# A fused attention and expert kernel: expert 0's second half takes its relus on the scalar engine, both halves are turned sooner, two small routing steps move

## The chip, the cores and the metric

One Trainium2 chip, of which the kernel uses one core. The metric is the time of one execution in microseconds on the device (us); lower is better. A core has a TensorE (PE: matrix products; PEld is its weight load), a VectorE (DVE), a ScalarE (ACT), a GpSimd (POOL) and a SyncE (SP), which here issues most transfers. Each engine takes its instructions in the order of its own queue.

## The reference, cut to what matters

```python
for t in range(S):                                   # B, H, S, D = 4, 8, 768, 48
    state = f[:, :, t, :, None] * state + np.einsum('bhd,bhe->bhde', k[:, :, t], v[:, :, t])
    y[:, :, t] = np.einsum('bhd,bhde->bhe', q[:, :, t], state)
x = y as (3072, 384)
h = x @ w_in                                         # (384, 2048)
x = (h - np.tanh(h)) @ w_out                         # (2048, 384)
out = x.copy()
xc = x[x @ w_skip > 0]                               # the rows that are computed
e_idx = np.argmax(xc @ w_gate, axis=1)               # one of 8 experts for each row
gate_w = the softmax probability of that expert
for e in range(8):
    h = np.maximum(xc[e_idx == e] @ w1[e], 0.0)      # (384, 1024), relu
    y[e_idx == e] = gate_w * (h @ w2[e])             # (1024, 384)
out[rows computed] = xc + y
```

## The kernel before, in words

Everything is fp32 in and out. The 3072 tokens are 24 blocks of 128 rows, or 12 pairs of blocks. Attention, the first product (`gemm1`), tanh and the second product (`gemm2`, L779) run interleaved for some 550 us. Their order is set by a planner that has a cost and a due time for every step, and for the last pairs by loops written by hand. In the last pair, the second block's last seven second products are kept for the end: the loop over `n` and `f` at `last = [route_now(...)...]` runs them with `gemm2(NB - 1, f, (1,))`. Each is three matmuls of 128x384.

**Routing.** As a block's rows are done they are copied from PSUM into a tile `pay` (`finish1`, L788). Scores for the eight experts and the skip score follow, and `place` (from L800) turns them into a row number of a buffer `xs` in HBM, in which every expert has a region: `choose` gives the one-hot row `oh`, the token's own number is copied from `ids` into `pay` (L803), two matmuls count the rows before this one (`pp`, L807 and L808, with `run` as the counts of all earlier blocks), `run` is increased by `oh` (L809), and on the DVE `sl`, `df` and `dst` (L813 to L821) make the address. The POOL then issues the scatter of `pay` into `xs` (L822). For the last two blocks, 22 and 23, `route_now` does the scores by transposes and products on the TensorE, between other work.

**Experts.** An expert takes up to 256 rows, read from `xs` into `xa` by `load_xa` (issued on SP, L996). Experts 1 to 7 split their weights and rows into a high and a low part, so that a product is three fast matmuls (`up` L1269, `down` L1293); the high part is a copy on the ScalarE (L352), the low part a subtract on the DVE or the POOL (L353). Expert 0 comes while the weights of expert 1 are being split, so it uses plain fp32 and goes in two halves of 128 rows, written (0,0) and (0,1):

- `half_turn` (L1013): three transposes (px, L1017) of the half's rows, then a copy to `xt` on the ScalarE (L1019).
- `half_up` (L1021), for eight f: three matmuls (L1027) into `eh`, a buffer of a pool `ph` that has two, then a relu on the DVE (L1030). The text calls such three matmuls an eh group.
- `half_down` (L1032), for eight f: a matmul of h with the second weight into `eo` (L1036).
- `deliver` (L1002): gate and residual on the DVE (`yo`, L1007), and a scatter into `out` (L999).

In time: half (0,0) is turned after the main stage's last product and after the copy of block 23 into `pay`; its eight half_ups have pieces of block 23's routing between them; `load_xa` for half (0,1) follows the last scatter. During the eight half_downs of (0,0), `split_raw(1, f)` splits expert 1's eight pieces of weight: eight copies on the ScalarE, six subtracts on the DVE, two on the POOL. Then come `deliver`, the turning of half (0,1), and its eight half_ups, with a `turn` of expert 1's rows (two transposes L1259 into a buffer `pt` of two, copy L1260, subtract on the DVE L1261) after f = 2, 4 and 6. From there expert follows expert.

Of the kernel before, what the change touches and what calls it, by code (L numbers as in the profile page):

```python
# [12 lines left out]
I32 = mybir.dt.int32  # L13
U32 = mybir.dt.uint32
AF = mybir.ActivationFunctionType
ALU = mybir.AluOpType
# [81 lines left out]
def decay_attention_moe_kernel(  # L98
# [14 lines left out]
    nc = tc.nc  # L113
    P = 128
    B, H, T, D = q.shape
    NT, DM = out.shape
# [8 lines left out]
    NF2 = F2 // P  # L125
# [58 lines left out]
    ids = cpool.tile([P, NU], I32, tag="ids", name="ids")  # L184
# [3 lines left out]
    run = cpool.tile([P, E], BF16, tag="run", name="run")  # L188
# [85 lines left out]
    def choose(pool, lg, tag):  # L274

        mx = pool.tile([P, 8], F32, tag="mx", name=f"mx{tag}")
        mi = pool.tile([P, 8], U32, tag="mi", name=f"mi{tag}")
        sm = pool.tile([P, 8], F32, tag="sm", name=f"sm{tag}")
        nm, rt, xf, sv = (sm[:, i : i + 1] for i in range(4))
        nc.vector.max(mx, lg[:, :E])  # L280
        nc.vector.tensor_scalar(nm, mx[:, 0:1], -1.0, None, op0=ALU.mult)
        ex = pool.tile([P, E], F32, tag="ex", name=f"ex{tag}")
        nc.scalar.activation(ex, lg[:, :E], AF.Exp, bias=nm, accum_out=sv)
        nc.vector.max_index(mi, mx, lg[:, :E])
        nc.vector.tensor_scalar(rt, lg[:, E : E + 1], 0.0, None, op0=ALU.is_gt)
        nc.vector.tensor_copy(xf, mi[:, 0:1])
        oh = pool.tile([P, E], BF16, tag="oh", name=f"oh{tag}")
        nc.vector.tensor_scalar(oh, iota8, xf, rt, op0=ALU.is_equal, op1=ALU.mult)
        return oh, rt, sv

    def gate_weight(gw, sv):
        nc.vector.tensor_scalar(gw, sv, 1e-9, None, op0=ALU.add)
        nc.vector.reciprocal(gw, gw)
# [10 lines left out]
    yp = pctx.enter_context(tc.tile_pool(name="yp", bufs=2, space=PSUM))  # L304
# [145 lines left out]
    def begun(u):  # L450
        blk, half = divmod(u, 2)
        return NF * blk - LEAD + 6 * half - (NF // 2 if 2 < blk <= LASTB else 0)
# [317 lines left out]
    def gemm2(blk, f, rows=(0, 1)):  # L770
        t = gt[blk, f]
        if f == first_f[blk]:
            for s in range(2):
                home, tag, w = (yp, "yp", 512) if blk in homes else (po_pool, "po", DM)
                po[blk, s] = home.tile([P, w], F32, tag=tag, name=f"po{blk}_{s}")[:, :DM]
        for s in rows:
            ss = slice(s * P, (s + 1) * P)
            for n, (a, w) in enumerate(((0, uhi), (0, ulo), (1, uhi))):
                nc.tensor.matmul(  # L779
                    po[blk, s], lhsT=t[:, a, ss], rhs=w[:, f], start=(f == first_f[blk] and n == 0),  # L780
                    stop=(f == last_f[blk] and n == 2),
                )
# [3 lines left out]
    def finish1(u):  # L786
        pt = pay[u] = rpool.tile([P, RW], F32, tag="pay", name=f"pay{u}", bufs=NPAY)
        nc.scalar.activation(pt[:, :DM], po[divmod(u, 2)], AF.Copy)  # L788

    def finish2(u):  # L790
        c, b = divmod(u, B)
        r0 = b * T + c * P
        nc.sync.dma_start(out[r0 : r0 + P, :], pay[u][:, :DM])

    def finish(blk, rows=(0, 1)):
        for s in rows:
            finish1(2 * blk + s)
            finish2(2 * blk + s)

    def place(pt, lg, u):  # L800

        oh, rt, sv = choose(rpool, lg, f"{u}")
        nc.vector.tensor_copy(pt[:, DM + 1 : DM + 2].bitcast(I32), ids[:, u : u + 1])  # L803
        yield
        yield
        pp = pa.tile([P, 512], F32, tag="pa", name=f"pp{u}")[:, :E]
        nc.tensor.matmul(pp, lhsT=tri_s, rhs=oh, start=True, stop=False)  # L807
        nc.tensor.matmul(pp, lhsT=ones, rhs=run, start=False, stop=True)  # L808
        nc.vector.tensor_tensor(run, run, oh, ALU.add)  # L809
        gate_weight(pt[:, DM : DM + 1], sv)  # L810
        yield
        sl = rpool.tile([P, E], F32, tag="sl", name=f"sl{u}")
        nc.vector.tensor_tensor(sl, pp, ebase, ALU.add)  # L813
        df = rpool.tile([P, 1], F32, tag="df", name=f"df{u}")
        s2 = rpool.tile([P, E], F32, tag="s2", name=f"s2{u}")
        nc.vector.tensor_tensor_reduce(
            out=s2, in0=sl, in1=oh, scale=1.0, scalar=float(OOB), op0=ALU.mult, op1=ALU.add, accum_out=df
        )
        c, b = divmod(u, B)
        di = dst[:, b * NCH + c : b * NCH + c + 1]  # L820
        nc.vector.scalar_tensor_tensor(out=di, in0=rt, scalar=-float(OOB), in1=df, op0=ALU.mult, op1=ALU.add)  # L821
        nc.gpsimd.indirect_dma_start(  # L822
            xs[:, :],
            bass.IndirectOffsetOnAxis(ap=di, axis=0),
            pt[:, :],
            None,
            bounds_check=E * NT - 1,
            oob_is_err=False,
        )
        yield  # L830

    def route(u):
        pt = pay[u]
        lg = rpool.tile([P, E + 1], F32, tag="lg", name=f"lg{u}")
        yield from dots(rpool, pt[:, :DM], f"{u}", wb, lg)
        yield from place(pt, lg, u)
# [130 lines left out]
    def split_raw(e, n):  # L967
        if e >= E:
            return
        raw = raws.pop((e, n))  # L970
        if n == 0:
            experts[e] = [wpool.tile([P, 2, KT, F2], F32R, tag="W", name=f"w1_{e}"), None]
        if n == NEC:
            experts[e][1] = wpool.tile([P, 2, NF2, DM], F32R, tag="W", name=f"w2_{e}")
        if n < NEC:
            a, w = experts[e][0], F2 // NEC
            fs = slice(n * w, (n + 1) * w)
            split(a[:, 0, :, fs], a[:, 1, :, fs], raw, nc.vector)
        else:
            a, r = experts[e][1], NF2 // NEC  # L980
            fs = slice((n - NEC) * r, (n - NEC + 1) * r)
            split(a[:, 0, fs], a[:, 1, fs], raw, nc.vector if e == 1 and n % 2 else nc.gpsimd)
        if e > 1:
            load_raw(e + 1, n)

    xas, xts, hts, eo = {}, {}, {}, {}
# [3 lines left out]
    def load_xa(e, rows=(0, 1)):  # L990
        if e < E:
            if e not in xas:
                xas[e] = epool.tile([P, 2, RW], F32, tag="xa", name=f"xa{e}", bufs=NXA)
            a, b = rows[0], rows[-1] + 1
            r0 = e * NT
            nc.sync.dma_start(xas[e][:, a:b], xs[r0 + a * P : r0 + b * P, :].rearrange("(s p) w -> p s w", p=P))  # L996
# [17 lines left out]
    def half_turn(e, s, pool, tag):  # L1014
        px = pool.tile([P, KT, P], F32, tag=tag, name=f"px{e}_{s}")
        for i in range(KT):
            nc.tensor.transpose(px[:, i], xas[e][:, s, i * P : (i + 1) * P], ident)  # L1017
        xts[e, s] = epool.tile([P, KT, P], F32, tag="xt", name=f"xt{e}_{s}")
        nc.scalar.activation(xts[e, s], px, AF.Copy)  # L1019

    def half_up(e, s, f):  # L1021

        ph = ph_pool.tile([P, P], F32, tag="ph", name=f"eh{e}_{s}_{f}")
        w = F2 // NEC
        n, fs = f * P // w, f * P % w
        for i in range(KT):
            nc.tensor.matmul(ph, lhsT=raws[e, n][:, i, fs : fs + P], rhs=xts[e, s][:, i], start=(i == 0), stop=(i == KT - 1))  # L1027
        if f % 4 == 0:
            hts[e, s, f // 4] = epool.tile([P, 4, P], F32, tag="h", name=f"h{e}_{s}_{f}", bufs=NH)
        nc.vector.tensor_scalar(hts[e, s, f // 4][:, f % 4], ph, 0.0, None, op0=ALU.max)  # L1030

    def half_down(e, s, f):  # L1032
        if f == 0:
            eo[e, s] = po_pool.tile([P, DM], F32, tag="po", name=f"eo{e}_{s}")
        n, m = divmod(f, NF2 // NEC)
        nc.tensor.matmul(  # L1036
            eo[e, s], lhsT=hts[e, s, f // 4][:, f % 4], rhs=raws[e, NEC + n][:, m], start=(f == 0), stop=(f == NF2 - 1)
        )
# [71 lines left out]
    for u in range(NU):  # L1110
        blk, half = divmod(u, 2)
        e = EARLIEST + 6 * u if u < FIRST else begun(u) - 8
# [116 lines left out]
    for n, f in enumerate(range(NF - SPLIT, NF)):  # L1229
        gemm2(NB - 1, f, (1,))  # L1230
        if n in (1, 3):
            next(last[0])
    finish(NB - 1, (1,))
    half_turn(0, 0, yp, "yp")
    next(last[0])
    for f in range(NF2):
        half_up(0, 0, f)
# [3 lines left out]
    for e in range(1, NXA):  # L1241
        load_xa(e)
    for f in range(NF2):
        half_down(0, 0, f)
        split_raw(1, f)
    deliver(0, (0,))
# [3 lines left out]
    pt_pool = mctx.enter_context(tc.tile_pool(name="ptp", bufs=2, space=PSUM))  # L1250
# [73 lines left out]
        nc.vector.tensor_copy(flag, fl)  # L1324
        yield

    half_turn(0, 1, pt_pool, "pt")
    for f in range(NF2):
        half_up(0, 1, f)
        if f in (2, 4, 6):  # L1330
# [8 lines left out]
    for g in range(NF2, E * NF2 + LAG):  # L1339
        e, f = divmod(g, NF2)  # L1340
# [276 lines left out]
```

## Time and profile before

| | us |
|---|---|
| median of three runs | 719.68 (718.21 to 721.0) |
| the profiled execution, its own time | 718.64 |
| its span | 716.8 |
| busy time: PE | 690.8 (96%) |
| busy time: PEld | 622.3 (87%) |
| busy time: DVE | 496.2 (69%) |
| busy time: ACT | 360.5 (50%) |
| busy time: POOL | 294.9 (41%) |

The span is what the hardware profiler saw between the first and the last instruction of one execution; what the execution takes beside it is 1.84 us. All times in rows are microseconds from the start of the span, unless marked ns. A matmul's end is modelled and overlaps the next one's start, so that starts are the better guide.

### The profile page before, as it was taken

To read this page: it belongs to the slowest core of one execution; us is meant where nothing else is said; L and a number is where in the kernel's file an instruction comes from. 1 tells how busy PE (TensorE), PEld (TensorE's weight loads), DVE (VectorE), ACT (ScalarE), POOL (GpSimd) and SP (SyncE) were. 2 spreads that over 40 slices of the span, in tenths; PEclk is the share of its full clock that TensorE was granted. 3 is DMA by queue.
4 is the path that set the end of the run, shared out by engine and by line. 5 is a ranking of instruction groups with operands and counts; after the bars stand their busy time and mean duration, and the time that the engine had idled before them with its cause. 6 is when DMAs were issued, how large, how long until landed. Compare 5 with 4: busy or idle time off the path is not lost.

```text
span 716.8 us, 15504 instructions
## 1 busy us (share of the span) xinstructions
PE 690.8 (96%) x5690; PEld 622.3 (87%) x5690; DVE 496.2 (69%) x1388; ACT 360.5 (50%) x882; POOL 294.9 (41%) x340
## 2 busy tenths in 40 slices
PE   7899989999999999999999999999999899999995
PEld 4688889988888888888889888999999689999995
DVE  3988997689878686784857669469784745555531
ACT  4877665564456453464454444443434435555530
POOL 4446444223333434334335334335543314555551
PEclk9999999999999999999999999999999999999998
DMA  9994345842232131222310120033003566666500
GB/s 224 231 258 128 123 165 145 251 88 46 54 76 56 35 88 32 54 51 55 68 24 29 40 58 17 7 122 117 13 29 104 179 222 227 218 213 216 176 16 25
DMA packets 147499, 76.71 MB, mean 107 GB/s; under 512 B 113288, under 2 KB 142617, under 8 KB 147286
## 3 DMA queue, kind: packets, MB, share of 16 engines
q1 hardware_dynamic: 142550, 64.18, 33.2%
q0 software_dynamic: 4768, 11.39, 4.4%
q8 instruction: 47, 0.77, 0.4%
q14 instruction: 38, 0.31, 0.1%
q10 hardware_dynamic: 96, 0.05, 0.0%
HBM read 61.60 MB, written 15.86 MB: 108 GB/s over the span
## 4 chain that ended last, share of the span: by engine, by line
PE 75%; DVE 6%; issue 5%; POOL 2%; ACT 1%; DMA 0%; POOLq 0%; ACTq 0%; DVEq 0%
PE po L779 24%; PE ph L737 22%; PE eh L1269 8%; PE eo L1293 8%; PE py L581 3%; PE ps L543 2%; POOL gs L762 2%; PE py L528 2%; PE eh L1027 1%; PE py L588 1%; PE pk L512 1%; PE pq L512 1%; DVE th L748 1%; PE eo L1036 1%; DVE kp L499 1%
## 5 line engine op out<-in xcount | busy, mean ns | idle before, releaser
L762 POOL TENSOR_TENSOR gs<-th,gs 128x256 fp32r<-128x256 f32 x190 | 162.3, 860 | 229.3 <-ACT gs L756 209.8
L779 PE MATMUL po<-uhi,gs 128*128 128x384 f32 x768 | 230.1, 347 | 3.9 <-POOL gs L762 2.1
L737 PE MATMUL ph<-xall,whi 128*128 128x256 f32 (+1 forms) x816 | 197.2, 331 | 1.7 <-DVE th L748 1.1
L779 PEld LDWEIGHTS po<-uhi,gs 128*128 128x128 f32 x768 | 140.9, 188 | 12.3 <-POOL gs L762 4.6
L737 PEld LDWEIGHTS ph<-xall,whi 128*128 128x128 f32 x816 | 138.2, 188 | 15.0 <-DVE th L748 2.2
L269 DVE CUSTOM_DVE_ANT_0 scr<-pay,wb 128x384 f32<-128x384 f32 x198 | 134.2, 678 | 8.6 <-ACT pay L788 4.4
L737 PE MATMUL ph<-xall,wlo 128*128 128x256 f32 (+1 forms) x408 | 133.9, 328 | 0.0
L756 ACT ACTIVATE gs<-th 128x256 fp32r<-128x256 f32 x192 | 79.2, 416 | 104.5 <-DVE th L748 76.4
L779 PE MATMUL po<-ulo,gs 128*128 128x384 f32 x384 | 129.3, 337 | 0.3 <-DVE ulo L415 0.3
L748 DVE TENSOR_TENSOR th<-ph,th 128x256 f32<-128x256 f32 x192 | 76.4, 417 | 68.6 <-ACT th L743 68.2
L743 ACT ACTIVATE th<-ph 128x256 f32<-128x256 f32 x192 | 68.6, 379 | 102.1 <-PE ph L737 71.2
L737 PEld LDWEIGHTS ph<-xall,wlo 128*128 128x128 f32 x408 | 77.0, 189 | 6.9
L779 PEld LDWEIGHTS po<-ulo,gs 128*128 128x128 f32 x384 | 72.5, 189 | 2.0 <-DVE ulo L415 0.6
L1269 PE MATMUL eh<-xt,w 128*128 128x256 f32 x504 | 69.8, 283 | 0.0
L1293 PE MATMUL eo<-w,h 128*128 128x384 f32 x336 | 69.4, 342 | 0.0
L1269 PEld LDWEIGHTS eh<-xt,w 128*128 128x128 f32 x504 | 67.1, 188 | 0.4
L1293 PEld LDWEIGHTS eo<-w,h 128*128 128x128 f32 x336 | 56.5, 188 | 0.0
L1278 DVE SCALAR_TENSOR_TENSOR h<-eh,h 128x256 fp32r<-128x256 f32 x56 | 23.7, 423 | 46.1 <-ACT h L1277 46.0
L1277 ACT ACTIVATE h<-eh 128x256 fp32r<-128x256 f32 x56 | 21.5, 385 | 62.6 <-PE eh L1269 62.5
L822 POOL DMA_INDIRECT xs<-pay,dst x24 | 26.9, 1122 | 63.1 <-DVE dst L821 44.7
L353 POOL TENSOR_TENSOR w<-r,w 128x768 fp32r<-128x768 f32 x24 | 44.4, 1850 | 14.5 <-ACT w L352 14.3
L999 POOL DMA_INDIRECT out_dram<-yo,xa x16 | 15.9, 992 | 67.2 <-DVE yo L1007 32.1
(197 smaller groups left out, 922.9 us busy)
## 6 DMA issues: line engine op xcount, KB each, us to landing
r<-in_moe_w_dram SPq DMA_DIRECT2D x56, 384.0 KB
stgu<-in_moe_w_out_dram SPq DMA_DIRECT2D x4, 1536.0 KB
f<-in_f_logit_dram SPq DMA_DIRECT2D x24, 192.0 KB
out_dram<-pay SPq DMA_DIRECT2D x24, 192.0 KB
k<-in_k_dram SPq DMA_DIRECT2D x22, 192.0 KB
q<-in_q_dram SPq DMA_DIRECT2D x22, 192.0 KB
v<-in_v_dram SPq DMA_DIRECT2D x22, 192.0 KB
xs<-zrow SPq DMA_DIRECT2D x2, 1544.0 KB
```

The source lines that it names most:

```text
L269: nc.vector.tensor_tensor_reduce(out=scr, in0=x, in1=wb[:, n], scale=1.0, scalar=0.0, op0=ALU.mult, op1=ALU.add, accum_out=lg[:, n : n + 1])
L353: eng.tensor_tensor(lo, raw, hi.bitcast(F32), ALU.subtract)
L737: nc.tensor.matmul(ph, lhsT=w[:, i, fs], rhs=x[:, i, a], start=(n == 0), stop=(n == 3 * KT - 1))
L743: nc.scalar.activation(th, ph, AF.Tanh)
L748: nc.vector.tensor_tensor(th, ph, th, ALU.subtract)
L756: nc.scalar.activation(t[:, 0], th, AF.Copy)
L762: eng.tensor_tensor(t[:, 1], th, t[:, 0].bitcast(F32), ALU.subtract)
L779: nc.tensor.matmul(po[blk, s], lhsT=t[:, a, ss], rhs=w[:, f], start=(f == first_f[blk] and n == 0), stop=(f == last_f[blk] and n == 2),)
L822: nc.gpsimd.indirect_dma_start(xs[:, :], bass.IndirectOffsetOnAxis(ap=di, axis=0), pt[:, :], None, bounds_check=E * NT - 1, oob_is_err=False,)
L1269: nc.tensor.matmul(ph, lhsT=a1[:, w, i, f * P : (f + 1) * P], rhs=xt[:, i, a], start=(n == 0), stop=(n == 3 * KT - 1))
L1278: nc.vector.scalar_tensor_tensor(out=h[:, 1], in0=ph, scalar=0.0, in1=h[:, 0].bitcast(F32), op0=ALU.max, op1=ALU.subtract)
L1293: nc.tensor.matmul(eo[e, s], lhsT=h[:, a, ss], rhs=a2[:, w, f], start=(f == 0 and n == 0), stop=(f == NF2 - 1 and n == 2))
```

## The change

1. In `place`, the copy of `ids` into `pay` stands before `choose` instead of behind it, and the addition to `run` stands behind the scatter instead of between the counting matmuls and the gate's weight.
2. In `half_up`, the relu of the second half (s = 1) is an activation on the ScalarE; the first half's stays on the DVE.
3. `half_turn(0, 0)` stands after the fifth of the seven second products that were kept, and no longer behind all and behind `finish`.
4. `half_turn(0, 1)` stands ahead of the last half_down of half (0,0), in the pool `yp` in place of `pt_pool`.

```diff
     def place(pt, lg, u):
 
+        nc.vector.tensor_copy(pt[:, DM + 1 : DM + 2].bitcast(I32), ids[:, u : u + 1])
         oh, rt, sv = choose(rpool, lg, f"{u}")
-        nc.vector.tensor_copy(pt[:, DM + 1 : DM + 2].bitcast(I32), ids[:, u : u + 1])
         yield
         yield
         pp = pa.tile([P, 512], F32, tag="pa", name=f"pp{u}")[:, :E]
         nc.tensor.matmul(pp, lhsT=tri_s, rhs=oh, start=True, stop=False)
         nc.tensor.matmul(pp, lhsT=ones, rhs=run, start=False, stop=True)
-        nc.vector.tensor_tensor(run, run, oh, ALU.add)
         gate_weight(pt[:, DM : DM + 1], sv)
...
             oob_is_err=False,
         )
+        nc.vector.tensor_tensor(run, run, oh, ALU.add)
         yield
...
-        nc.vector.tensor_scalar(hts[e, s, f // 4][:, f % 4], ph, 0.0, None, op0=ALU.max)
+        if s:
+            nc.scalar.activation(hts[e, s, f // 4][:, f % 4], ph, AF.Relu)
+        else:
+            nc.vector.tensor_scalar(hts[e, s, f // 4][:, f % 4], ph, 0.0, None, op0=ALU.max)
...
         gemm2(NB - 1, f, (1,))
         if n in (1, 3):
             next(last[0])
+        if n == 4:
+            half_turn(0, 0, yp, "yp")
     finish(NB - 1, (1,))
-    half_turn(0, 0, yp, "yp")
...
     for f in range(NF2):
+        if f == NF2 - 1:
+            half_turn(0, 1, yp, "yp")
         half_down(0, 0, f)
         split_raw(1, f)
...
-    half_turn(0, 1, pt_pool, "pt")
     for f in range(NF2):
         half_up(0, 1, f)
```

In the instruction order three places change. On the TensorE, at the end of the main stage (po is the second product's sum, px_0 half (0,0)'s transposes), before:

```order
L779 MATMUL po_1_7086<-uhi,gs_13_7412 128x384
L779 MATMUL po_1_7086<-uhi,gs_14_7431 128x384
L779 MATMUL po_1_7086<-ulo,gs_14_7431 128x384
L779 MATMUL po_1_7086<-uhi,gs_14_7431 128x384
L779 MATMUL po_1_7086<-uhi,gs_15_7450 128x384
L779 MATMUL po_1_7086<-ulo,gs_15_7450 128x384
L779 MATMUL po_1_7086<-uhi,gs_15_7450 128x384
L1017 MATMUL px_0_7521<-ident,xa_7397 128x128 x3
L807 LDWEIGHTS tri_s
```

and with the change:

```order
L779 MATMUL po_1_7086<-uhi,gs_13_7412 128x384
L1017 MATMUL px_0_7512<-ident,xa_7397 128x128 x3
L779 MATMUL po_1_7086<-uhi,gs_14_7431 128x384
L779 MATMUL po_1_7086<-ulo,gs_14_7431 128x384
L779 MATMUL po_1_7086<-uhi,gs_14_7431 128x384
L779 MATMUL po_1_7086<-uhi,gs_15_7450 128x384
L779 MATMUL po_1_7086<-ulo,gs_15_7450 128x384
L779 MATMUL po_1_7086<-uhi,gs_15_7450 128x384
L807 LDWEIGHTS tri_s
```

The transposes of half (0,0) moved ahead of the last two second products. On the TensorE again, at the end of half (0,0) (eo_0 is its sum, px_1 the transposes of half (0,1)), before:

```order
L1036 MATMUL eo_0_7627<-r_6_6536,h_0_4_7605 128x384 x2
L1036 MATMUL eo_0_7627<-r_7_6538,h_0_4_7605 128x384 x2
L1017 MATMUL px_1_7667<-ident,xa_7397 128x128 x3
L1027 MATMUL eh_1_0_7673<-xt_1_7671,r_0_6524 128x128 x3
L1027 MATMUL eh_1_1_7679<-xt_1_7671,r_0_6524 128x128 x3
```

and with the change:

```order
L1039 MATMUL eo_0_7627<-r_6_6536,h_0_4_7605 128x384 x2
L1039 MATMUL eo_0_7627<-r_7_6538,h_0_4_7605 128x384
L1017 MATMUL px_1_7651<-ident,xa_7397 128x128 x3
L1039 MATMUL eo_0_7627<-r_7_6538,h_0_4_7605 128x384
L1027 MATMUL eh_1_0_7673<-xt_1_7655,r_0_6524 128x128 x3
L1027 MATMUL eh_1_1_7679<-xt_1_7655,r_0_6524 128x128 x3
```

The transposes went ahead of the last half_down. On the ScalarE, in the same stretch (w are expert 1's split weights, xt_1 the turned rows of half (0,1), h_1 its relus, xt_7689 the turned rows of expert 1), the piece of the difference:

```order
-L352 ACTIVATE w_1_7642<-raw_7456 128x768 x4
-L1019 ACTIVATE xt_1_7671<-px_1_7667 128x384
-L1260 ACTIVATE xt_7689<-pt_0_7690 128x256
...
+L352 ACTIVATE w_1_7642<-raw_7456 128x768 x3
+L1019 ACTIVATE xt_1_7655<-px_1_7651 128x384
+L352 ACTIVATE w_1_7642<-raw_7456 128x768
+L1031 ACTIVATE h_1_0_7677<-eh_1_0_7673 128x128
+L1031 ACTIVATE h_1_0_7677<-eh_1_1_7679 128x128
+L1031 ACTIVATE h_1_0_7677<-eh_1_2_7684 128x128
+L1266 ACTIVATE xt_7689<-pt_0_7690 128x256
```

One of the eight copies of expert 1's weights now stands behind the copy of the turned rows, and the relus follow, with the copies of `turn` between them. On the DVE the same eight relus are gone from between yo and the subtracts of `turn`. The orders of the POOL and of SP are the same.

## Rows read from the trace of the kernel before

**Rows 1.** The page, busy time of each engine: busy us, share of span, instructions
```profile
PE 690.8 (96%) x5690; PEld 622.3 (87%) x5690; DVE 496.2 (69%) x1388; ACT 360.5 (50%) x882; POOL 294.9 (41%) x340
```

**Rows 2.** PE's waits, 540 to 717 us: us in total, times, longest
```profile
PE eh L1027 <- DVE h L1030: 1.8, 1, 1.8
PE eh L1027 <- ACT xt L1019: 1.2, 2, 0.6
```

**Rows 3.** Table by stretch: length; busy (instructions) of PE, PEld, DVE, ACT, POOL; PEclk, DMA, GB/s
```profile
584.00:717.00 133.00, 124.21 (x879) 123.48 (x877) 62.21 (x126) 61.56 (x122) 59.34 (x40) 0.99 0.49 159
```

**Rows 4.** PE's timeline, 553 to 585 us: start, duration, instruction [idle before <- releaser]
```profile
555.71 0.34 PE L779 MATMUL po<-uhi,gs 128*128 128x384 f32 x1
555.89 0.49 PE L1017 MATMUL px<-ident,xa 128*128 128x128 f32 x3
...
557.01 0.94 PE L1027 MATMUL eh<-xt,r 128*128 128x128 f32 x6 [0.60 <-ACT xt L1019]
...
564.42 5.33 PE L1036 MATMUL eo<-r,h 128*128 128x384 f32 x16
569.59 0.49 PE L1017 MATMUL px<-ident,xa 128*128 128x128 f32 x3
570.71 1.60 PE L1027 MATMUL eh<-xt,r 128*128 128x128 f32 x12 [0.63 <-ACT xt L1019]
574.14 0.94 PE L1027 MATMUL eh<-xt,r 128*128 128x128 f32 x6 [1.83 <-DVE h L1030]
...
575.13 1.50 PE L1027 MATMUL eh<-xt,r 128*128 128x128 f32 x12
576.47 0.38 PE L1259 MATMUL pt<-ident,xa 128*128 128x128 f32 x2
```

**Rows 5.** ACT's timeline, 553 to 580 us
```profile
556.09 0.49 ACT L788 ACTIVATE pay<-po 128x384 f32<-128x384 f32 x1 [0.88 <-PE po L779]
...
560.45 5.96 ACT L352 ACTIVATE w<-raw 128x768 fp32r<-128x768 f32 x8
570.16 0.49 ACT L1019 ACTIVATE xt<-px 128x384 f32<-128x384 f32 x1 [3.76 <-issue]
```

**Rows 6.** DVE's timeline, 560 to 585 us
```profile
561.25 0.14 DVE L803 COPY pay<-ids 128x1 int32<-128x1 int32 x1
...
564.83 8.53 DVE L353 TENSOR_TENSOR w<-raw,w 128x768 fp32r<-128x768 f32 x6
```

**Rows 7.** SP's timeline, 535 to 570 us: when it issues the loads of xa
```profile
546.97 0.33 SPq L996 DMA_DIRECT2D xa<-xs  x1
...
566.01 1.32 SPq L996 DMA_DIRECT2D xa<-xs  x3
```

**Rows 8.** Line L1017's instructions: duration in ns, first and last start
```profile
L1017 PEldq EVENT_SEMAPHORE  x1: 51/51/51, 568.4 to 568.4; - x1
```

**Rows 9.** POOL's timeline, 545 to 572 us: the last two scatters
```profile
558.10 1.00 POOL L822 DMA_INDIRECT xs<-pay,dst  x1 [10.05 <-DVE dst L821]
563.60 0.98 POOL L822 DMA_INDIRECT xs<-pay,dst  x1 [4.50 <-DVE h L1030]
```

**Rows 10.** Line L822, at 558 to 559 us and at 563 to 565 us: issue to landing
```profile
DMA to landing us min/median/max: 4.7/4.7/4.7
...
DMA to landing us min/median/max: 2.4/2.4/2.4
```

**Rows 11.** PE's waits, 150 to 549 us, the largest: us in total, times, longest
```profile
PE pk L512 <- DVE kp L499: 1.4, 4, 0.7
```

**Rows 12.** Relus on the DVE and the ScalarE: line L1030 (ns), the page's costliest groups
```profile
L1030 DVE TENSOR_SCALAR h<-eh x16: 273/290/293, 558.0 to 579.2; 128x128 f32<-128x128 f32 x16
...
L1277 ACT ACTIVATE h<-eh 128x256 fp32r<-128x256 f32 x56 | 21.5, 385 | 62.6 <-PE eh L1269 62.5
```

**Rows 13.** Table by stretch, columns as in rows 3
```profile
558.00:560.00 2.00, 2.00 (x19) 1.90 (x18) 0.80 (x4) 0.49 (x1) 1.00 (x1) 1.00 1.10 385
562.00:564.00 2.00, 2.00 (x21) 2.00 (x20) 1.14 (x8) 2.00 (x4) 0.40 (x1) 1.00 0.01 4
```

## The prediction, made before the changed kernel was run

> **What bounds the kernel now.** First the busy shares: the TensorE works 96% of the span [rows 1], so the time is its work plus its idle gaps, and the change alters no product. Next, who waited for whom: after 540 us only three TensorE waits touch the lines of this change, 1.83 us for a relu of the DVE and twice 0.6 us for the turned rows of expert 0 [rows 2]. The table by stage tells whether time saved there is kept: from 584 us on nothing but products runs, 124 us of busy TensorE in a stretch where the wait view names no wait at all [rows 3]. What the TensorE reaches earlier before 584 us, it therefore ends earlier, as long as weights and rows come in time.
>
> The TensorE's own timeline gives three gaps [rows 4]. **Gap A**: the transposes of half (0,0) (px, L1017) start at 555.89, behind the last product of the main stage; the ScalarE copies them behind its copy of pay [rows 5], and the first eh starts at 557.01, after 0.60 us of waiting for that copy. **Gap B**: px of half (0,1) starts at 569.59, its copy at 570.16 [rows 5], eh at 570.71: 1.12 us from px to eh. **Gap C**: the third eh group of half (0,1), f = 2, starts at 574.14. There are two ph buffers, so f = 2 waits for relu f = 0. One group takes 0.67 us (two in 575.13 to 576.47), so its own time was 570.71 + 1.34 = 572.05: 2.09 us late. The DVE timeline shows why [rows 6]: six splits of expert 1's weights fill 564.83 to 573.36, then come yo and the relus that the TensorE wants. The ScalarE meanwhile ended its eight split copies at 566.41, and its next instruction is the copy at 570.16 [rows 5].
>
> **Part 1, half (0,0) turned two products sooner.** px now stands two second products ahead of the end of the main stage. A product is three matmuls, and one comes every 0.18 us (555.71 to 555.89 [rows 4]), so px and its copy get 1.06 us more to be ready. The px work itself stays on the TensorE; it only changes places with the products. The copy, under 0.5 us, lies beside the two products: the ScalarE sat idle for 0.88 us before 556.09 [rows 5]. The rows are there, their load was issued at 546.97 [rows 7]. So eh starts as soon as the products are done, and the 0.60 us of waiting go; half_down, at 564.42 before, starts at 563.82. What is late next: pay of block 23 (L788) reads the last product, which now ends three transposes later (0.11 us each, a sixth of a group's 0.67, so 0.33), so its copy, its transposes and its gate products come 0.33 later against a half that runs 0.60 earlier. They stand between eh groups; what they can cost is that the TensorE meets one of them before it is ready, at most 0.33, and part 3 takes two DVE instructions out of the same chain. I carry the 0.60.
>
> **Part 2, half (0,1) turned before the last half_down.** Seven of eight half_downs are 7/8 of 5.17 us (564.42 to 569.59), so px could start at 563.82 + 4.52 = 568.34. It must find its rows: their load is issued at 566.01 [rows 7], and the weight queue's wait for it stands at 568.4 [rows 8]. This load waits for the last scatter, issued at 563.60 [rows 9] and landed 2.4 us later [rows 10]; that scatter waited in turn for the one before it, issued at 558.10 and landed 4.7 us later, at 562.8 [rows 9, 10]. So the rows stay at about 568.4 even if the routing's chain is shorter. Behind px the TensorE has one half_down (0.65 us); px to eh stays 1.12. So eh starts at 568.4 + 1.12 = 569.52; at best 569.46 (no wait for rows), at worst 569.72 (0.2 us of queue and semaphore on top). Parts 1 and 2 together make it 1.0 to 1.25 earlier than 570.71; I take 1.15. The eighth split copy of expert 1 now lies behind this copy on the ScalarE (an eighth of 5.96 us, so about 569.5 to 570.3, done before the first relu at 570.6); the DVE's subtract of it is the last of six that ended at 573.36, and so does not wait.
>
> **Part 3, routing.** The copy of ids and the add into run leave the chain from gate to scatter: the copy takes 0.14 us [rows 6], the add is of the same small kind, in 24 blocks. In the main stage I cost them at nothing: the TensorE's largest waits between 150 and 549 us, 1.4 us in all, are for kp and not for routing [rows 11]. If moved DVE instructions delay a th or kp, or help one, the bound is that size: plus or minus 0.5 us, range only. At the end it shortens blocks 22 and 23 by about 0.3 us; the landing of the scatter before the last hides that, as shown (at most 0.3 of gain, if the landing at 562.8 moves with its issue).
>
> **Part 4, relus of half (0,1) on the ScalarE.** Eight relus leave the DVE's queue and wait no more for the splits. The trace has no 128x128 relu on the ScalarE. Nearest rows: the relu of the later experts, 128x256, takes 0.385 [rows 12]; the copy of 128x384 takes 0.49 [rows 5]. The line through both gives 0.28 at 128 columns, an estimate; 0.385 bounds it from above, and below 0.26 nothing more is gained. The DVE's own is 0.29 [rows 12]. The loop of two buffers is then: eh group 0.94 (start to modelled end) + 0.08 to the ScalarE (px ends 570.08, copy starts 570.16) + 0.28 + 0.06 back (570.65 to 570.71) = 1.36 against 1.34 for two groups. So f = 2 stalls 0.02 us, at 0.385 some 0.13; the later pairs have two transposes between them (1.34 + 2 x 0.11 = 1.56) and stall at neither. Gap C shrinks from 2.09 to about 0.04: 2.05 gained. The Trainium skill speaks against this edit: "ScalarE: Activation LUTs", section "Rules for kernel authors", says to put relu on VectorE, up to about three times faster per element in bf16. Here the data are fp32 from PSUM, and the line through the rows puts both engines within a few per cent; a ScalarE so much slower is the second rival, priced there from rows.
>
> A new wait: there are two pt buffers, so the third pair of transposes of expert 1 (L1259) waits for the DVE's subtract of the first. On the DVE that subtract now stands right behind the splits and yo: splits until 573.36 at the latest; yo and a relu of 0.29 were done by 574.14 before, so yo by 573.85; and a subtract of even twice a relu, 0.6, ends at 574.45. The TensorE gets there at 569.56 + 1.36 + 0.67 + 2 x 1.56 = 574.7, so no stall, with 0.25 us or more to spare. Behind the waiting transposes stand only the last eh group and half_down. Expert 1's first product comes after eight more half_downs, 5 us later, long after its splits.
>
> **Sum** on the profiled execution (span 716.8, own time 718.64): 1.15 + 2.05 = 3.2 less, 715.4. This execution stands 1.0 below the median of the three runs shown, 719.68; taking the same 3.2 off the median gives **716.5**. A difference below 0.5%, 3.6 us, is what a measurement here can hardly tell from none, so the forecast lies just inside that.
>
> **Rivals.**
> *The scatter moves the bound (slower).* px(0,1) now stands in TensorE's queue ahead of the last half_down, and TensorE takes its queue in order: if the rows are late, everything stops with it. If the last scatter and the load behind it both took 4.7 us like the scatter before, they would land at 563.6 + 4.7 + 4.7 = 573.0; eh at 574.2, f = 2 at 575.5 against 574.14: 1.4 slower, 721.1. It decides from a landing after 571.6 on. For it: that first scatter needed 4.7 while the DMA engines were full. Against it: the share was 1.10 at 558 to 560 and 0.01 at 562 to 564, and the weights' loads are over by then [rows 13]. Chance 0.05.
> *The ScalarE's relu becomes the bound.* At 0.87, three times the DVE's 0.29, the loop were 0.94 + 0.08 + 0.87 + 0.06 = 1.95: f = 2 loses 0.61, and two later pairs 1.95 - 1.56 = 0.39 each, 1.4 in all: 717.9. The rule of the Trainium skill on relu ("ScalarE: Activation LUTs", "Rules for kernel authors") would have it this way. The same ScalarE does 256 columns in 0.385 [rows 12], which speaks against it. Chance 0.08.
> *The turns bring nothing.* The rows land a microsecond later, or block 23's routing, 0.33 behind, pushes the chain to the scatter: eh of (0,1) starts near 570.5 as before, only part 4 counts, 2.05 and little more: 717.6. For it: the xa load sits on two landings that no part of the change shortens. Against it: the last scatter waited for the landing, not for the DVE. Chance 0.09.
> *More comes.* The routing edit takes 1 us out of the main stage's waits or lets the scatter land sooner: 1.0 more, 715.5. Chance 0.10.
>
> **How the numbers follow.** Forecast 0.68, rivals 0.05, 0.08, 0.09 and 0.10. The terms alone leave 716.0 to 717.0; medians of three runs that spread 718.2 to 721.0 add about 1 on either side. The range reaches from the last rival to the second, 714.6 to 718.7, and leaves out the slower one. Faster by over 0.5% needs less than 716.1: a third of the forecast (0.23) and nearly all of the last rival (0.09), 0.32. Slower by over 0.5% needs 723.3: a later landing than the first rival's, or a main stage put out of step by the moved DVE instructions, 0.04. Within 0.5%: 0.64.
>
> **What would show it.** First eh of (0,0) right behind the last product (no wait for xt); px(0,1) between half_downs with a weight wait until about 568.4 and eh at 569.5; ScalarE relus of 0.28 and f = 2 within 0.15 us of its two groups; the TensorE's waits for xt and relu after 540 us, 3.0 us now, down to under 0.4; from 584 us on the same timeline 3.2 us sooner. Wrong it is if the landing of xa moves by over 0.5 us, if a relu takes over 0.45, if the third turn's transposes wait for the DVE, or if the stretch up to 555 us changes by more than 0.5.

## The result, and the profile after

The change is faster by more than the range allowed: 713.84 us median of six executions (712.34 to 715.35) against 720.34 of six of the kernel before (718.21 to 722.44). The ratio is 0.9908, 95% interval 0.9884 to 0.9933, or 6.5 us. The forecast was 716.5 us, the range began at 714.6. The profiled execution of the change took 713.45 us, its span is 711.6: 5.2 us less than the span before.

The page of the changed kernel, its first lines:

```profile
span 711.6 us, 15497 instructions
## 1 busy us (share of the span) xinstructions
PE 690.3 (97%) x5690; PEld 623.3 (88%) x5690; DVE 494.0 (69%) x1380; ACT 363.7 (51%) x890; POOL 294.7 (41%) x340
```

The TensorE's work is what it was (690.8 before [rows 1]); what went is idle time. The TensorE's waits from 530 us to the end of the program, in the change:

```profile
PE po L779 <- ACT gs L756: 0.4, 1, 0.4
PE pp L807 <- DVE oh L288: 0.3, 1, 0.3
```

and before, 540 us to the end, below [rows 2]:

```profile
PE po L779 <- ACT gs L756: 0.4, 1, 0.4
PE pp L807 <- DVE pay L803: 0.3, 1, 0.3
```

The first row stood in the list before too. The second is the routing's: before, the counting matmul waited 0.3 us for the copy of ids (L803), a wait on a line of this change that the prediction did not count; with the copy moved it waits as long for the one-hot row. The waits for xt and for the relu [rows 2] are gone. The TensorE's timeline of the change, 546 to 582 us:

```profile
552.88 0.49 PE L1017 MATMUL px<-ident,xa 128*128 128x128 f32 x3
...
554.09 0.34 PE L779 MATMUL po<-uhi,gs 128*128 128x384 f32 x1
...
554.34 0.91 PE L1027 MATMUL eh<-xt,r 128*128 128x128 f32 x6
...
561.67 4.68 PE L1039 MATMUL eo<-r,h 128*128 128x384 f32 x14
566.47 0.55 PE L1017 MATMUL px<-ident,xa 128*128 128x128 f32 x3
566.86 0.81 PE L1039 MATMUL eo<-r,h 128*128 128x384 f32 x2
567.60 2.27 PE L1027 MATMUL eh<-xt,r 128*128 128x128 f32 x18
...
572.83 0.38 PE L1265 MATMUL pt<-ident,xa 128*128 128x128 f32 x2
...
578.59 3.68 PE L1275 MATMUL eh<-xt,w 128*128 128x256 f32 x26
```

Against [rows 4]: eh of half (0,0) follows 0.25 us after the start of the last product, where it was 1.30 with px between. Three eh groups of half (0,1) run in one row of 18 matmuls, where the third came 3.43 us after the first. And the whole picture is some 2 us early: the last product starts at 554.09 with three transposes ahead of it that stood behind it before, at 555.71. That is 1.6 earlier, 2.0 with the transposes' slots, before anything that the prediction credited has begun.

The ScalarE and the DVE in the change, 549 to 575 us and 557 to 575 us:

```profile
553.41 0.49 ACT L1019 ACTIVATE xt<-px 128x384 f32<-128x384 f32 x1
...
567.06 0.49 ACT L1019 ACTIVATE xt<-px 128x384 f32<-128x384 f32 x1 [4.08 <-PE px L1017]
567.45 0.84 ACT L352 ACTIVATE w<-raw 128x768 fp32r<-128x768 f32 x1
568.58 0.28 ACT L1031 ACTIVATE h<-eh 128x128 f32<-128x128 f32 x1 [0.29 <-PE eh L1027]
```

```profile
562.08 9.25 DVE L353 TENSOR_TENSOR w<-raw,w 128x768 fp32r<-128x768 f32 x6
571.25 0.60 DVE L1007 SCALAR_TENSOR_TENSOR yo<-eo,xa 128x384 f32<-128x384 f32 x1
571.78 0.75 DVE L1267 TENSOR_TENSOR xt<-pt,xt 128x256 fp32r<-128x256 f32 x2
```

The relu takes 0.28 us, the estimate; the split copy between the turned rows and the first relu ended 0.29 us ahead of it. The DVE's subtracts for expert 1 come after splits and yo, the first two done by 572.53, ahead of the third turn's transposes at 572.83, which need only the first of them.

To set stretches of executions side by side, this table takes the starts of the same TensorE instructions in each trace: a matmul of a second product near 150 us (149.93 before), one of a first product near 545 us (544.97), the first eh of half (0,0), the first and the third eh of half (0,1), and the last product of expert 7 (707.87).

| us, from start to start | before | change |
|---|---|---|
| start of the span to product at 150 | 149.93 | 150.00 |
| I: to the product near 545 | 395.04 | 393.01 |
| II: to eh of (0,0) | 12.04 | 11.33 |
| III: to eh of (0,1) | 13.70 | 13.26 |
| IV: to its third eh | 3.43 | 1.44 |
| V: to the last product | 133.73 | 133.64 |

Stretches II to V give 3.2 us, what the prediction had summed. Stretch I gives 2.0 more, where it had put nothing.

### The profile page after: what moved, and what is told of

Same layout as the page of the kernel before. It is cut to its first block, busy times and chain, and to the rows that moved or that the text cites. A ratio compares the mean times of both kernels' runs of the same rounds, so it can differ in the third digit from the quotient of the medians.

```text
span 711.6 us, 15497 instructions
## 1 busy us (share of the span) xinstructions
PE 690.3 (97%) x5690; PEld 623.3 (88%) x5690; DVE 494.0 (69%) x1380; ACT 363.7 (51%) x890; POOL 294.7 (41%) x340
## 4 chain that ended last, share of the span: by engine, by line
PE 79%; DVE 6%; issue 5%; POOL 3%; DMA 3%; ACT 2%; SPq 0%; POOLq 0%; ACTq 0%; DVEq 0%
PE po L779 25%; PE ph L737 24%; PE eh L1275 9%; PE eo L1299 8%; PE ps L543 3%; PE py L581 3%; POOL gs L762 2%; PE py L528 2%; DMA f<-in_f_logit_dram 1%; PE py L588 1%; PE eh L1027 1%; PE pk L512 1%; PE pq L512 1%; PE eo L1039 1%; DVE th L748 1%
## 5 line engine op out<-in xcount | busy, mean ns | idle before, releaser
L269 DVE CUSTOM_DVE_ANT_0 scr<-pay,wb 128x384 f32<-128x384 f32 x198 | 133.5, 674 | 8.6 <-ACT pay L788 4.4
L748 DVE TENSOR_TENSOR th<-ph,th 128x256 f32<-128x256 f32 x192 | 76.4, 417 | 71.0 <-ACT th L743 70.1
```

Source lines behind the costliest of these rows:

```text
L269: nc.vector.tensor_tensor_reduce(out=scr, in0=x, in1=wb[:, n], scale=1.0, scalar=0.0, op0=ALU.mult, op1=ALU.add, accum_out=lg[:, n : n + 1])
L748: nc.vector.tensor_tensor(th, ph, th, ALU.subtract)
```

## The experiments

Two theories stood first. A: the gain beyond the forecast is the routing edit's, in the main stage. B: it is chance of an execution's start, or comes from the turns and relus in a way not yet seen. The first four kernels split the change.

**Routing edit alone.** Point 1 of the change, nothing else.

```diff
+        nc.vector.tensor_copy(pt[:, DM + 1 : DM + 2].bitcast(I32), ids[:, u : u + 1])
         oh, rt, sv = choose(rpool, lg, f"{u}")
-        nc.vector.tensor_copy(pt[:, DM + 1 : DM + 2].bitcast(I32), ids[:, u : u + 1])
...
-        nc.vector.tensor_tensor(run, run, oh, ALU.add)
         gate_weight(pt[:, DM : DM + 1], sv)
...
+        nc.vector.tensor_tensor(run, run, oh, ALU.add)
         yield
```

> The routing edit alone (copy of ids ahead of choose, addition to run behind the scatter); turns and relus as before. Theory A (the gain beyond the forecast comes from the routing edit in the main stage: DVE instructions of the 24 blocks stand better against the transposes of k and against the counting products): 1.5 to 3.5 us faster than before, the TensorE's waits for kp between 150 and 549 us down from 1.4 to about 0.5, the last product of the main stage about 2 us sooner, and all three gaps for xt and relu of expert 0 still there. Theory B (the gain beyond the forecast is chance in the start of an execution, or comes from the turns and relus): within 0.5 us of before.

Measured: 718.28 us against 720.16, ratio 0.998 (0.9961 to 0.9999). Its trace: stretch I 393.03, II to V as before (12.05, 13.63, 3.47). The TensorE's wait list from 150 to 549 us:

```profile
PE pk L512 <- DVE kp L499: 0.5, 1, 0.5
PE py L528 <- DVE A L565: 0.2, 1, 0.2
```

The four waits for kp of 1.4 us [rows 11] are one of 0.5. Gone, too, is the second row of the list before, which [rows 11] does not show ("issue": the engine waited for nothing that the profile shows):

```profile
PE po L779 <- issue: 0.5, 1, 0.5
```

These two rows make 1.4 of the 2.0 us. Theory A holds for the stretch; the median moved by 1.9, within its interval of the 2.0.

**Turns and relus without the routing edit.** Points 2 to 4 of the change; against the whole change:

```diff
-        nc.vector.tensor_copy(pt[:, DM + 1 : DM + 2].bitcast(I32), ids[:, u : u + 1])
         oh, rt, sv = choose(rpool, lg, f"{u}")
+        nc.vector.tensor_copy(pt[:, DM + 1 : DM + 2].bitcast(I32), ids[:, u : u + 1])
...
+        nc.vector.tensor_tensor(run, run, oh, ALU.add)
         gate_weight(pt[:, DM : DM + 1], sv)
...
-        nc.vector.tensor_tensor(run, run, oh, ALU.add)
```

> The turns and the relus without the routing edit. Theory A: the forecast sum alone, 3.0 to 3.4 us faster than before, main stage as before (kp waits 1.4 us). Theory B: 5.5 to 6.5 us faster, as the whole change.

Measured: 717.28, ratio 0.9961 (0.9942 to 0.998), 2.9 us of the medians. Stretches I to IV: 394.91, 11.35, 13.53, 1.44. The main stage is as before, and the end gives 2.9. Theory B falls as far as it put the rest on the turns and relus.

**Relus alone.**

```diff
-        nc.vector.tensor_scalar(hts[e, s, f // 4][:, f % 4], ph, 0.0, None, op0=ALU.max)
+        if s:
+            nc.scalar.activation(hts[e, s, f // 4][:, f % 4], ph, AF.Relu)
+        else:
+            nc.vector.tensor_scalar(hts[e, s, f // 4][:, f % 4], ph, 0.0, None, op0=ALU.max)
```

> Only the relus of half (0,1) on the ScalarE. Both theories: f = 2 of half (0,1) starts 1.34 to 1.45 us after f = 0, where it was 3.43; a relu takes 0.28 us; the time from the first eh of half (0,1) to 584 us and the whole 2.0 us shorter. If the ScalarE's relu were three times the DVE's (0.87 us), 0.6 to 0.7 us.

Measured: 718.99, ratio 0.9975 (0.9955 to 0.9995), 1.2 us of the medians, 1.8 by the ratio. Stretch IV is 1.44, 1.99 less than before; I, II and III are within 0.2 of before. As expected.

**Turns alone.**

```diff
+        if n == 4:
+            half_turn(0, 0, yp, "yp")
     finish(NB - 1, (1,))
-    half_turn(0, 0, yp, "yp")
...
+        if f == NF2 - 1:
+            half_turn(0, 1, yp, "yp")
         half_down(0, 0, f)
...
-    half_turn(0, 1, pt_pool, "pt")
```

> Only the two turns moved. First eh of half (0,0) 0.6 us sooner after the last product, eh of half (0,1) about 1.1 us sooner; but the relus of half (0,1) still stand behind the DVE's splits and yo, which do not move or move by at most 0.6 us: f = 2 at 573.5 to 574.1 as before. So by the forecast's working 0 to 0.6 us faster, not the 1.15 that the turns were given; if the sum of parts holds, 1.1.

Measured: 721.93, ratio 1.0022 (0.9999 to 1.0045): no faster. Stretch II gains its 0.72, III loses 0.86 (14.56), IV gains 0.58 (2.85), together 0.4, as the cap by the relus foretold; but III lost where it was to win. Row of its timeline:

```profile
573.91 0.55 PE L1017 MATMUL px<-ident,xa 128*128 128x128 f32 x3 [1.36 <-DMA xa<-xs]
```

The TensorE stood 1.36 us in front of px for rows that had not landed; the scatter before the last had taken 5.6 us to land here, the last 2.8. That is the slower rival of the prediction at work in a small way. In the kernel with relus and turns the same wait was 0.34 us. How long the scatters take differs from execution to execution (4.7 in the trace before [rows 10], 5.0 in the change).

**Which half of the routing edit.** Two kernels that each do one of the moves. The copy of ids:

```diff
+        nc.vector.tensor_copy(pt[:, DM + 1 : DM + 2].bitcast(I32), ids[:, u : u + 1])
         oh, rt, sv = choose(rpool, lg, f"{u}")
-        nc.vector.tensor_copy(pt[:, DM + 1 : DM + 2].bitcast(I32), ids[:, u : u + 1])
```

> Only the copy of ids stands ahead of choose. In the traces so far the routing edit shortens the stretch from 150 us to the end of the main stage by 1.9 us, without it that stretch is unchanged. If the copy is the part (it stood between the one-hot row and the counting matmuls, which the trace of before shows released by it): about 1.9 us less in that stretch, and the 0.45 us of TensorE idle at 542 us gone. If the addition to run is the part: under 0.3 us.

The addition to run:

```diff
-        nc.vector.tensor_tensor(run, run, oh, ALU.add)
         gate_weight(pt[:, DM : DM + 1], sv)
...
+        nc.vector.tensor_tensor(run, run, oh, ALU.add)
         yield
```

> Only the addition to run stands behind the scatter. If this addition is the part (it waited on the DVE for the counting matmuls, with all of the DVE's queue behind it): 1 to 1.9 us less from 150 us to the end of the main stage, the waits for kp shorter, the idle at 542 us still there. If the copy of ids is the part: under 0.3 us.

Measured: 718.89 and 718.84 us, one execution each beside a median of 721.25, which tells nothing apart. Stretch I does: 394.84 with the copy moved, 393.13 with the addition moved. The addition is the part, with 1.9 of the 2.0 us. The idle at 542 us, which the expectation had put on the copy, stays with the copy moved and goes with the addition moved.

A part of the reason shows in a view that the prediction did not read, the DVE's own waits. Before, 150 to 549 us, the third row of the list:

```profile
DVE run L809 <- PE pp L808: 7.1, 7, 2.1
```

and in the change the two that are left for these matmuls:

```profile
DVE sl L812 <- PE pp L808: 1.2, 2, 1.0
...
DVE th L748 <- PE pp L808: 0.5, 1, 0.5
```

The addition writes `run`, which the second counting matmul reads, so the DVE held its whole queue until the TensorE came to that matmul: seven times, 7.1 us, the longest 2.11. What that one cost, on the DVE before, 162 to 170 us:

```profile
162.65 0.16 DVE L809 TENSOR_TENSOR run<-run,oh 128x8 bf16<-128x8 bf16 x1 [2.11 <-PE pp L808]
...
165.29 0.35 DVE L473 CAST lfs<-f 128x384 fp32r<-128x384 f32 x1
...
166.16 2.36 DVE L499 TENSOR_TENSOR kp<-k,kp 128x384 f32<-128x384 f32 x1
```

on the POOL, and on the TensorE:

```profile
165.57 1.06 POOL L822 DMA_INDIRECT xs<-pay,dst  x1 [3.52 <-DVE okd L647]
166.66 1.43 POOL L762 TENSOR_TENSOR gs<-th,gs 128x256 fp32r<-128x256 f32 x2
...
168.57 0.65 PE L512 MATMUL pk<-ident,kp 128*112 128x128 f32 x4 [0.30 <-DVE kp L499]
```

In the change kp is done by 167.74, and its transposes start at 168.18 without a wait; the DVE and the POOL there:

```profile
165.24 1.02 DVE L473 CAST lfs<-f 128x384 fp32r<-128x384 f32 x1 [1.18 <-issue]
...
167.19 0.55 DVE L499 TENSOR_TENSOR kp<-k,kp 128x384 f32<-128x384 f32 x1
...
165.28 1.56 POOL L762 TENSOR_TENSOR gs<-th,gs 128x256 fp32r<-128x256 f32 x2
```

The cast ahead of kp starts at the same time in both, 165.29 and 165.24, and kp itself starts 1.0 us later in the change: the DVE had made up the 2.11 us by then. What the wait did move is the address of this block's scatter, and with it the POOL: its two subtracts (`gs`) behind the scatter start at 166.66 before, beside kp, and at 165.28 in the change, beside the cast. These DVE instructions are longer beside the POOL's subtracts (the numbers are in the last section): kp 2.36 against 0.55 us, the cast 1.02 against 0.35. In sum kp ended 0.8 us later. In all seven traces whose addition waits one kp takes 2.36 to 2.38 us; in the other seven the longest takes 1.09.

**The wait without the place.** To tell the wait from the addition's place in the DVE's order, a kernel with the addition where it was and two buffers for the counts:

```diff
+    run2 = cpool.tile([P, E], BF16, tag="run2", name="run2")
...
+        nonlocal run, run2
...
-        nc.vector.tensor_tensor(run, run, oh, ALU.add)
+        nc.vector.tensor_tensor(run2, run, oh, ALU.add)
+        run, run2 = run2, run
```

> The kernel before, but the counts alternate between two buffers: the addition stays where it was in the DVE's order, and writes the buffer that the counting matmuls do not read, so it has nothing to wait for. If the wait of the DVE for the counting matmuls (7.1 us in 7 waits between 150 and 549 us in the trace of before) is what cost the main stage 1.9 us: that wait row gone and the stretch from 150 us to the end of the main stage 1.7 to 2.0 us shorter, waits for kp 0.5 us, as in the kernel that only moved the addition. If it is the place of the addition in the DVE's order or in the chain to the scatter: under 0.3 us.

Measured: 720.61 against 720.52, ratio 1.0009 (0.9993 to 1.0025): no gain that the medians show. In its trace the DVE waits for no counting matmul at the addition any more, but sl waits 0.9 us for one; stretch I is 393.59, 1.45 us shorter, 0.66 of it up to 200 us, where 1.7 to 2.0 or under 0.3 were expected. The TensorE's waits there:

```profile
PE pk L513 <- DVE kp L500: 1.0, 3, 0.7
PE po L780 <- issue: 0.4, 1, 0.4
```

Laid side by side, the TensorE's starts show at which places the time is won. The second column is how long the addition waited in the block just ahead, in the trace before:

| TensorE late before at, us | addition's wait, us | won with the addition moved | won with two buffers |
|---|---|---|---|
| 168, for kp | 2.11 | 0.63 | 0.63 |
| 207, for kp | 0 | 0.23 | 0.04 |
| 294 and 337, for kp | 0 | 0.21 | 0.10 |
| 488 to 491 | 0.20 | 0.25 | 0.31 |
| 542, "issue" | 0 | 0.61 | 0.03 |
| elsewhere in stretch I | | 0.0 | 0.35 |

So the wait is worth 0.9 us of the 1.9, at two of its seven places; behind the other five, up to 1.51 us long, the TensorE lost nothing. The other 1.0 us comes where the addition waited for nothing, and needs it out of its place. For the largest piece of that, at 542 us, the traces show a step between: one of the products for the scores (scr, L269) took 1.57 us on the DVE before and 0.56 in the change,

```profile
533.38 1.57 DVE L269 CUSTOM_DVE_ANT_0 scr<-pay,wb 128x384 f32<-128x384 f32 x1
...
531.98 0.56 DVE L269 CUSTOM_DVE_ANT_0 scr<-pay,wb 128x384 f32<-128x384 f32 x1
```

and so it is in every trace: 1.57 or 1.58 us in the eight with the addition in its place, this kernel's among them, 0.56 in the six with it moved. From there to 542 us the DVE is 0.8 us further on against the TensorE. Why the place changes that one instruction was not tried, nor where the 0.35 us of this kernel come from. That the median did not follow the stretch is not settled: this execution reached the product near 150 us at 153.93, 4.0 late (2.4 at 50 us, 5.6 at 62), and whether the additional buffer or chance does that was not tried. Its TensorE was busy for 1.28 and 1.56 us of the two stretches of 2 us from 52 to 56, and from 58 to 62 its granted clock read 0.50, the lower of the two levels (1.2 GHz), where the trace before reads 1.00 from 50 to 65.

**The whole change but the addition.** Against the change:

```diff
+        nc.vector.tensor_tensor(run, run, oh, ALU.add)
         gate_weight(pt[:, DM : DM + 1], sv)
...
-        nc.vector.tensor_tensor(run, run, oh, ALU.add)
         yield
```

> The whole change, but the addition to run stands where it stood before. Main stage as in the kernel before (2.0 us longer than in the change, to 0.2), the wait of the DVE for the counting matmuls back at about 7 us; the end of the program as in the change, but for the rows of half (0,1), whose scatters come later against the TensorE, so that its transposes wait 0.3 to 1.4 us for them as in the two kernels without the routing edit.

Measured: 716.41 us, one execution. Stretches I to V: 394.80, 11.32, 13.20, 1.44, 133.63. The addition's 7.1 us of DVE wait is back, and so is stretch I to 0.2. The expectation on the rows of half (0,1) missed: III is 13.20, and the transposes waited no longer than in the change.

**The place of the second turn.** The whole change, the transposes behind the last half_down.

```diff
-        if f == NF2 - 1:
-            half_turn(0, 1, yp, "yp")
         half_down(0, 0, f)
+        if f == NF2 - 1:
+            half_turn(0, 1, yp, "yp")
         split_raw(1, f)
```

> The whole change, but the transposes of half (0,1) stand behind the last half_down (the order on the ScalarE stays). If their place ahead of it gives what the forecast gave it: the first eh of half (0,1) comes 0.4 to 0.6 us later against the start of half (0,0)'s first half_down (6.4 us with the transposes behind, 5.93 in the change), all else as the change. If the rows land too late for it to matter: no difference.

Measured: 715.37, one execution. From first half_down to eh of (0,1) 6.23 us, in the change 5.93: the place is worth 0.30, not 0.4 to 0.6. Its timeline:

```profile
568.44 0.49 PE L1017 MATMUL px<-ident,xa 128*128 128x128 f32 x3
569.51 2.27 PE L1027 MATMUL eh<-xt,r 128*128 128x128 f32 x18 [0.58 <-ACT xt L1019]
```

The wait for xt is back (0.63 in [rows 4]). In the change px could start at 561.67 + 7/8 of 5.16 (the eight half_downs here), 566.19, and started at 566.47: it waited for its rows for 0.28, where the prediction had 0.06.

**The change again, and the kernel before against itself.**

> The whole change once more, beside runs of before on the same chip. By the traces' stretches (2.0 us main stage, 0.6 first turn, 0.5 second turn, 2.05 relus): 5.2 us faster, 0.9928. If the first measurement's 6.5 us hold, 0.991, and 1.3 us of it are in no stretch yet seen.

> The kernel before against itself. Its ratio is 1 within 0.2%. If the first 15 us of an execution differ by themselves (each of the four traces of other kernels so far reaches 17 us between 1.1 and 3.4 us later than the trace of before, with the same program up to there), this trace reaches 17 us 1 to 3 us later too and all its later stretches stay at that distance, within 0.3 us.

> The whole change a third time, to settle how far the measured gain lies from the 5.2 us that the stretches of the traces add up to. If the difference is only the chance of the first 100 us of the executions drawn: the three measurements spread about 0.9928, and this one lies at 0.992 to 0.9935. If the change has 1.3 us more that no stretch shows: 0.990 to 0.9915 again, and the trace reaches 150 us sooner than most traces of other kernels.

Measured: the change 0.9906 (0.9881 to 0.9931) and 0.9938 (0.9916 to 0.996), the kernel before 0.999 (0.9973 to 1.0007) against itself. The second measurement is near the 0.991 that would have stood for the whole 6.5 us, the third just above the 0.992 to 0.9935 that stood for the stretches alone. The three measurements of the change give 6.5, 6.1 and 4.2 us of the medians. Its three traces give stretches I to IV alike: 393.01, 393.00, 393.01; 11.33, 11.33, 11.32; 13.26, 13.22, 13.29; 1.44 each. So the stretches say 5.2 us each time, and what differs is the start: the three reached the product near 150 us at 150.00, 149.58 and 151.54. The kernel before, at 149.93 in its first trace, was there at 153.83 in the second:

```profile
153.83 0.44 PE L779 MATMUL po<-uhi,gs 128*128 128x384 f32 x1
```

with stretch I 394.96 and II to V as in the first, to 0.35. At 17 us it was 3.7 late, a little over the 1 to 3 expected. Over the thirteen traces with the same program up to there this start spreads from 149.58 to 154.22. 5.2 us lie within each of the three intervals; that the change had another 1.3 us no run showed.

## Why the prediction was wrong

- **Part 1, first turn:** right. 0.71 us against 0.60 taken, with block 23's routing no obstacle.
- **Part 2, second turn:** right in mechanism and, with part 1, in sum: II and III give 0.71 + 0.44 = 1.15, the number taken. px started when its rows had landed. Its own share is 0.30 (the kernel with px behind), of a forecast 0.55. Without the other edits it can lose: 0.86 in the kernel with turns alone.
- **Part 4, relus:** right. 1.99 us against 2.05, f = 2 stalled 0.10 (1.44 against 1.34), not 0.02. A relu took 0.28 us on the ScalarE and 0.29 on the DVE [rows 12], fp32 from PSUM, and the ScalarE was idle. The trace so differs from the Trainium skill's rule on relu ("ScalarE: Activation LUTs", "Rules for kernel authors"), which prefers VectorE and gives its factor for bf16. The new wait of the third turn's transposes did not bind; the subtract that they need was done at 572.19, 0.6 us ahead.
- **Part 3, routing: the step that failed.** "In the main stage I cost them at nothing", with plus or minus 0.5 us as a bound for the range. It measured 2.0 us, 1.9 from the addition alone. The step read only the TensorE's waits, found 1.4 us for kp [rows 11], and called that "not for routing". Three things it did not have. The DVE's own wait list had a row of 7.1 us for the addition; that wait was worth 0.9 us, 0.6 of it through the POOL's subtracts and a slow kp. The addition's place was worth another 1.0, also where it waited for nothing. And one of the two largest pieces, 0.6 us at 542, was no wait for kp at all: it stood in the same list as "issue", one row below the kp row that was read. Even the 7.1 us would not have given the size, as five of the seven waits cost the TensorE nothing. One sign that the prediction had named for being wrong came true: the stretch up to 555 us changed by more than 0.5.
- **The rivals.** "More comes" named the routing edit and gave it 1 us, 715.5, at 0.10; it was this one, twice as large. The slower one showed only in the kernel with turns alone.
- **The range.** 3.2 + 2.0 = 5.2 us off the 719.68 that was shown makes 714.5, just under its lower end of 714.6; the measured 713.84 lies 0.7 below that, less than the medians of the change differ among themselves (713.84, 715.11, 716.39). A half-width of 0.5 us for two moved DVE instructions in each of 24 blocks was the term that was too narrow. That the first median fell below the range and those of the later measurements (715.11, 716.39) inside it is in part luck: it fits the spread of the start, which is seen only in the profiled executions. The 2.0 us of the main stage are no luck; all three traces of the change have them.

## What to carry to other kernels

When an instruction is moved, read the waits of its own engine, not only those of the engine that bounds: a small instruction that waits for the bounding engine holds everything behind it, and what that delays shows under other names. The length of such a wait is not its price: 7.1 us in seven waits cost 0.9 here, all of it at two of them. Work on an idle engine at the same price (relu 0.28 against 0.29 us) is worth the queue that it no longer stands behind, here 2.0 us for eight relus. A transpose that is moved ahead of work in TensorE's queue pays only if its rows have landed: 0.3 us won here, 0.9 lost where they were late.

## What the runs showed of the hardware

The first 100 us of an execution vary by themselves, most of it in the first 20: with the same program the traces reach a product near 150 us at 149.58 to 154.22 us, and keep that distance to the end (the kernel before 153.83 against 149.93, its last product 4.2 later). That is more than any single edit of this change is worth, and stretches between named instructions, alike to 0.07 us in the change's three traces (to 0.35 in the two of the kernel before), told apart what medians could not. And the same DVE instruction varies with what the POOL does beside it. In each of the fourteen traces kp, an elementwise instruction of 128x384 in fp32, runs 22 times on the DVE. It took 0.54 to 0.56 us whenever no elementwise instruction of the POOL (a TENSOR_TENSOR, such as the subtracts of gs) ran during it, 13 or 14 times in each trace, and a scatter's issue beside it changed nothing (five times before, at most 0.56). It took 0.78 to 2.38 us the other 8 or 9 times. Not every DVE instruction does so: th (the subtract behind tanh, L748), 128x256, which takes one of its inputs from PSUM, took 0.40 to 0.43 us with the POOL's work beside it (28 times before) or without. What decides how much longer an instruction gets the traces do not show. So the addition's wait, which put a scatter's address off by 1.4 us, could change the time of DVE instructions that it does not touch.
